# Row sums of seven groups of heads: 32x32 transposes and sums along columns on VectorE in place of a ones matmul

## The chip, the cores and the metric

The kernel runs on one core of one Trainium2 chip. The metric is the device time of one execution in microseconds (us). Of the core's engines five matter here: PE (TensorE, matrix products), ACT (ScalarE, exponentials and copies), DVE (VectorE, additions), POOL (GpSimd, used here to issue DMAs, some of which add to what lies at their destination) and SP (SyncE, which issues the other DMAs). Each engine takes its instructions in the order in which the program issues them.

## The reference

The output mixes attention (A) with a sparse part (B), token by token, by a gate g. Cut to attention, which the change concerns, it is:

```python
def _A_ref(x, wqkv, wo):
    H = 32; Dh = D // H                     # S = 2048 tokens, D = 1024, Dh = 32
    q, k, v = ...                           # x @ wqkv, split into heads
    scores = jnp.einsum("bhqd,bhkd->bhqk", q, k) * (Dh ** -0.5)
    p = _softmax(scores, axis=-1)
    o = jnp.einsum("bhqk,bhkd->bhqd", p, v)
    return o.transpose(...).reshape(B, S, D) @ wo

return g * a + (1 - g) * b
```

The kernel doesn't divide p by its sum. It computes exp(scores), multiplies that with v, and divides afterwards: for each head and each of the 2048 queries it needs the sum of the exponentials over all 2048 keys, the row sum. The change is about how these row sums come about.

## The kernel before

Up to about 628 us of the span the kernel computes q, k, v and part B; from about 1626 us on it multiplies with wo and mixes. Between lies the loop over the 32 heads, eight groups of four (G = 8), which the change touches.

**Tiles of a head.** The keys of a head lie on partitions, 128 at a time: NT = 16 tiles kt, each 128 keys by 2048 queries. `scores` (L1285) makes four products of 512 queries for a tile, each in one bank of `ring`, seven banks of PSUM used in turn. ACT takes 1 to 4 banks at a time and writes exp into P[h, kt] in SBUF (L1294). `pv` (L1306) multiplies P with v on PE. The order is written out: `batches` gives in turn a batch of 9 or 10 products of scores and then products with v some tiles behind. A head has seven batches, and only the third has ten products. A step k = h * 16 + kt stands for one tile; `at(step, f, ...)` puts a piece of other work behind the scores of that step, and in a step such pieces come before `presum`.

**Row sums.** They are sums over partitions and tiles. `presum` adds the tiles of a head into ACC[h] on DVE, and an addition (`add`, L1347) is always two instructions of 1024 columns. Three pairs of tiles, (0, 2), (4, 6) and (8, 10), are first added by a DMA that POOL issues (`accumulate`, L1336: the second onto the first); the sums of the pairs go into ACC by `add_pair` at steps 12 and 17 of the head (counted from its first step) and by a merge at step 21, that is, in tile 5 of the next head. So a head has twelve additions.

For groups 0 to 5 (`FOURS = 6`) the merge and the folds bring four heads into one tile T of 128 partitions, 32 for each head. `merge4` adds the last pair: for the first head of a group straight into T, for the other three its own quarter into T and the rest into ACC. `fold4` and `fold4_end` add the other quarters onto that quarter by DMAs. Then one `head_sums` multiplies T with a matrix of ones on PE (`rowsum`, L1319, into a bank of the ring), ACT copies the sums out (`norm_sums`, L1417), and DMAs carry them to DRAM (SMD) and back into R, 128 partitions by 64 (`load_r`). `norm_r` takes the reciprocal (L1429), multiplies with the gate and writes RD. Groups 6 and 7 do the same for two heads at a time with `merge_even`, `merge_odd`, `fold_even` and `fold_odd`, whose second head also needs two additions for one; heads 30 and 31 have their sums from ACC alone. T is the tile rb0, which the end of the kernel uses again.

**Places of P.** P tiles lie in places that are used again and again: 13 at first, 11 from step 328 (head 20, tile 8), 10 from step 443 (head 27, tile 11), for the others are needed for loads of wo and of other data (`PLACES`). `p_tile` gives each new tile the place that is due first (`until`): 5 steps after a plain tile, 10 after the second of a pair, 14 after the first. ACT can write a tile only when the tile before in its place has been read for the last time: by PE for the product with v, by DVE for the addition, by the DMA of its pair.

Of the kernel before, what the change touches and what calls it, by code (L numbers as in the profile page):

```python
# [19 lines left out]
H = 32  # L20
# [12 lines left out]
def gated_mha_peer_kernel(ctx, tc, xT, wqkv, wv, wo, wq, k12, ug, v, out):  # L33
# [37 lines left out]
    ones4 = const.tile([128, 32], F32, name="ones4")  # L71
    for t, heads in ((ones2, 2), (ones4, 4)):
        nc.vector.memset(t, 0.0)
        for i in range(heads):
            m, w = 128 // heads, 32 // heads
            nc.vector.memset(t[m * i:m * i + m, w * i:w * i + w], 1.0)


    const.tile([128, 120], F32, name="fill")
# [1074 lines left out]
    PLACES = (13, 0), (11, 20 * NT + 8), (10, 27 * NT + 11)  # L1154
# [3 lines left out]
    def p_tile(h, kt):  # L1158
# [4 lines left out]
        i = min((i for i in range(n) if i not in (8, 9) or k < H * NT - 8), key=lambda i: until[i])  # L1163
# [3 lines left out]
                      (wk, f"P{i}") if i < 10 else (keep, ("vhl", "wo_raw2", "wo_raw3")[i - 10]))  # L1167
# [155 lines left out]
    def presum(h, kt):  # L1323
# [14 lines left out]
    def pair(h, i):  # L1338
        return P[h, PAIRS[h == H - 1][i][0]]
# [29 lines left out]
    FOURS = 6  # L1369

    def quarter(i):
        return slice(32 * i, 32 * i + 32)

    def others(q):
        return [quarter(i) for i in range(4) if i != q]

    def merge4(h):
        q = h % 4
        if q == 0:
            add(T, ACC.pop(h), pair(h, -1))  # L1380
        else:
            mine = quarter(q)
            add(T[mine], ACC[h][mine], pair(h, -1)[mine])
            add_pair(h, -1)

    def fold4(h):
        q = h % 4
        if q == 0:
            nc.gpsimd.dma_start(T[up], T[low], accum_op=OP.add)
        else:  # L1390
            a, b, c = others(q)
            nc.gpsimd.dma_start(ACC[h][a], ACC[h][b], accum_op=OP.add)
            nc.gpsimd.dma_start(T[quarter(q)], ACC[h][c], accum_op=OP.add)

    def fold4_end(h):
        q = h % 4
        src = T[quarter(1)] if q == 0 else ACC.pop(h)[others(q)[0]]
        nc.gpsimd.dma_start(T[quarter(q)], src, accum_op=OP.add)

    def head_sums(h, heads=1):  # L1400
        i, = ring_banks(1)
        for ins in rowsum(ring[:, i, :], T if heads > 1 else ACC.pop(h),
                          ones={1: ones, 2: ones2, 4: ones4}[heads]):
# [434 lines left out]
```

## Time and profile before

| | us |
|---|---|
| three runs | 1811.03, 1811.66, 1812.90 (median 1811.66) |
| the execution profiled | 1811.52 |
| its span, first to last instruction | 1809.7 |
| loop over the heads in that span | about 628 to 1626 |

A row of the profile names the line, the engine, the operation and the tiles (written<-read), its shape and count, then the busy time in us, the mean duration of one in ns, and behind a bar the idle time of the engine before such instructions and what ended it. In the timeline a row gives start and duration in us of some instructions in succession that are alike, and in square brackets the idle time before. In rows of stretches the numbers after the length are busy us and counts of PE, PE's weight loads, DVE, ACT and POOL, then the granted clock of PE, the share of the DMA engines and GB/s. A row of waits says who waited for whom, us in total, how often, and the longest. `rb` is T, `wo_raw` and `vhl` are places of P that lie in tiles of these names.

### The profile page before, as it was taken

Reading aid. Unit: us, or ns where it says so; the run is one execution under the profiler, and the core shown is the slowest. Engines: PE = TensorE matmul, PEld = TensorE weight load, DVE = VectorE, ACT = ScalarE, POOL = GpSimd, SP = SyncE. Lnnn points to the kernel's source line nnn. Section 1 sums busy time; section 2 is a strip of 40 time slices with the busy share of each in tenths; the row PEclk is TensorE's granted clock in tenths of the full one; section 3 lists DMA queues with packets and bytes.
Section 4 is the critical chain, followed back from the end, with each engine's and each line's share of the span. In section 5 each row is a group of like instructions: output and inputs, shape, how many; then the busy total and the mean of one; then the engine's idle time right before and its main releaser. Section 6 shows DMA issues by size and latency. Waiting matters only on the chain.

```text
span 1809.7 us, 28079 instructions
## 1 busy us (share of the span) xinstructions
PE 1801.0 (100%) x10631; PEld 1137.0 (63%) x10631; DVE 1503.6 (83%) x1673; ACT 1221.5 (67%) x1613; POOL 262.4 (15%) x314
## 2 busy tenths in 40 slices
PE   9999999999999999999999999999999999999999
PEld 7877777788888745555454555454555545547887
DVE  7868776358988689999989999999899989995674
ACT  4434321211233399999999999999999999993221
POOL 0212000026401211111211111111112010101000
PEclk9999999999999999999999999999999999999999
DMA  6887888723238699999999999999999998957851
GB/s 234 243 284 248 272 267 295 258 79 106 82 129 276 225 217 185 195 198 199 191 202 205 208 209 194 206 184 208 200 202 198 207 199 189 201 130 228 280 168 58
DMA packets 132225, 364.74 MB, mean 202 GB/s; under 512 B 17540, under 2 KB 57876, under 8 KB 106168
## 3 DMA queue, kind: packets, MB, share of 16 engines
q0 software_dynamic: 22064, 136.07, 39.3%
q1 hardware_dynamic: 89864, 190.94, 35.3%
q10 hardware_dynamic: 20160, 35.92, 7.0%
q8 instruction: 84, 1.38, 0.3%
q14 instruction: 53, 0.43, 0.1%
HBM read 169.14 MB, written 72.10 MB: 133 GB/s over the span
## 4 chain that ended last, share of the span: by engine, by line
PE 97%; DMA 2%; ACT 0%; issue 0%; DVE 0%; SPq 0%; ACTq 0%; DVEq 0%
PE ring L1285 29%; PE o L1306 26%; PE bk L157 13%; PE bk L713 10%; PE pa L157 6%; PE bk L760 5%; PE bk L928 2%; PE bk L313 2%; PE pa L1582 2%; PE bk L493 1%; PE bk L397 1%; PE pa L1589 1%; DMA wraw<-in_wqkv 1%; DMA smd<-ssb 1%; PE ring L1319 0%; ACT P L1294 0%
## 5 line engine op out<-in xcount | busy, mean ns | idle before, releaser
L1294 ACT ACTIVATE P<-ring 128x512 f32<-128x512 f32 (+3 forms) x995 | 807.8, 932 | 12.9 <-PE ring L1285 6.7
L1347 DVE TENSOR_TENSOR acc<-acc,P 128x1024 f32<-128x1024 f32 x516 | 596.0, 1219 | 30.5 <-ACT P L1294 29.8
L1306 PE MATMUL o<-P,V 128*32 128x512 f32 (+1 forms) x3896 | 408.7, 540 | 0.0
L1285 PE MATMUL ring<-Q,K 98*128 98x512 f32 x1024 | 269.4, 406 | 0.0
L1285 PE MATMUL ring<-z,z 98*128 98x512 f32 x1020 | 267.5, 406 | 0.1
L1285 PEld LDWEIGHTS ring<-Q,K 98*128 98x128 f32 x1024 | 182.7, 188 | 121.4 <-ACT P L1294 42.1
L1285 PEld LDWEIGHTS ring<-z,z 98*128 98x128 f32 x1020 | 182.1, 188 | 114.6 <-issue 39.5
L1306 PEld LDWEIGHTS o<-P,V 128*32 128x32 f32 x3896 | 108.4, 109 | 203.8 <-issue 179.7
L1336 POOL DMA_DIRECT2D P<-P x78 | 81.4, 1043 | 496.5 <-PE o L1306 190.5
L1347 DVE TENSOR_TENSOR acc<-acc,wo_raw 128x1024 f32<-128x1024 f32 x118 | 139.0, 1220 | 13.4 <-ACT wo_raw L1294 13.4
L1294 ACT ACTIVATE wo_raw<-ring 128x512 f32<-128x512 f32 (+3 forms) x134 | 119.6, 988 | 0.0
L242 ACT ACTIVATE hi<-bk 128x512 fp32r<-128x512 f32 x40 | 23.7, 594 | 116.4 <-PE bk L713 102.2
L713 PE MATMUL bk<-xh,e 128*128 128x512 f32 x384 | 94.2, 394 | 0.0
L713 PE MATMUL bk<-xl,e 128*128 128x512 f32 x384 | 92.2, 389 | 0.0
L713 PEld LDWEIGHTS bk<-xh,e 128*128 128x128 f32 x384 | 71.0, 188 | 22.0 <-issue 3.4
L1347 DVE TENSOR_TENSOR acc<-P,P 128x1024 f32<-128x1024 f32 x60 | 70.8, 1221 | 16.2 <-ACT P L1294 15.9
L255 DVE TENSOR_TENSOR lo<-bk,hi 128x512 fp32r<-128x512 f32 x40 | 27.6, 690 | 67.5 <-ACT hi L242 62.7
L713 PEld LDWEIGHTS bk<-xl,e 128*128 128x128 f32 x384 | 72.1, 188 | 15.0
L103 DVE TENSOR_TENSOR e<-wraw,e 128x512 fp32r<-128x512 f32 (+3 forms) x64 | 54.6, 861 | 27.0 <-ACT e L102 26.7
L102 ACT ACTIVATE e<-wraw 128x512 fp32r<-128x512 f32 (+3 forms) x64 | 44.7, 705 | 37.7 <-DMA wraw<-in_wqkv 22.0
L157 PE MATMUL bk<-xh,e 128*128 128x512 f32 x288 | 68.5, 393 | 0.0
L1306 PE MATMUL o<-wo_raw,V 128*32 128x256 f32 (+1 forms) x632 | 66.6, 496 | 0.0
(300 smaller groups left out, 2377.4 us busy)
## 6 DMA issues: line engine op xcount, KB each, us to landing
P<-P POOLq DMA_DIRECT2D x78, 1024.0 KB, 12.0
wqt<-in_wq SPq DMA_DIRECT2D x26, 1024.0 KB
wraw<-in_wqkv SPq DMA_DIRECT2D x30, 512.0 KB
vhl<-P POOLq DMA_DIRECT2D x13, 1024.0 KB, 13.5
rb<-acc POOLq DMA_DIRECT2D x36, 256.0 KB, 7.2
qdh<-hi ACTq DMA_DIRECT2D x32, 256.0 KB
qdl<-lo ACTq DMA_DIRECT2D x32, 256.0 KB
kdh<-hi ACTq DMA_DIRECT2D x32, 256.0 KB
```

The costliest lines, as they stand in the source:

```text
L102: nc.scalar.activation(hi, src, AF.Copy)
L103: (on or nc.vector).tensor_tensor(out=lo, in0=src, in1=hi.bitcast(F32), op=OP.subtract)
L157: nc.tensor.matmul(ps, self.a[a][i][:, k, :], self.b[b][j][k], start=(not first and k == 0 and i == j == 0), stop=(k == HC - 1 and i == 1))
L313: nc.tensor.matmul(ps[32 * quad:32 * quad + 32, :], kpad[:, quad % 2, i, :], t[:, quad, :], start=(i == 0), stop=(i == 3))
L713: nc.tensor.matmul(ps, t[:, kc // HC, a, kc % HC], x_at(b, n, kc), start=first, stop=last)
L760: nc.tensor.matmul(ps, x_at(a, t // 4, kc)[:, tok], b, start=first, stop=last)
L928: nc.tensor.matmul(p, x_at(a, t // 4, kc)[:, tok], b, start=first, stop=last)
L1285: on_ring(nc.tensor.matmul(ring[:, i, :], K[:98, kt * 128:(kt + 1) * 128], Q[:98, qc * 512:(qc + 1) * 512], start=True, stop=True), i)
L1294: on_ring(nc.scalar.activation(P[h, kt][:, q0 * 512:(q0 + m) * 512].rearrange("p (a m) -> p a m", a=m), ring[:, i:i + m, :], AF.Exp, scale ...
L1306: nc.tensor.matmul(O[h][32 * qc:32 * qc + 32, c0:c1], Vt[g][:, kt, 32 * j:32 * j + 32], p[:, qc * 512 + c0:qc * 512 + c1], start=(kt == 0) ...
L1336: nc.gpsimd.dma_start(P[h, b], P[h, a], accum_op=OP.add)
L1347: nc.vector.tensor_add(out[:, c], a[:, c], b[:, c])
```

## The change

Groups 0 to 6 (`FOURS = 7`) no longer use a ones matmul. Each head is merged into its own ACC with one addition (`merge`), at the same step as before. POOL then issues three DMAs in turn: partitions 64 to 127 are added onto 0 to 63 (`fold64`, step 23 of the head), 32 to 63 onto 0 to 31 (`fold32`, step 27), and the 32 partitions that remain are copied into the head's quarter of T (`collect`, step 31). After the last head of a group, in four successive steps from step 36 of that head, that is, in tiles 4 to 7 of the head after the next, `sum32` transposes a quarter of T's columns in blocks of 32x32 on VectorE (reading T in steps of 64 elements) and adds each 32 columns, which gives R in the layout that `load_r` brought before, without a way over DRAM. `norm_r` follows at step 40; it was at step 52 for groups 0 to 5 and at step 41 for group 6. The matrix `ones4` goes.

Since ACC is held longer, every third head has its ACC in what was the place P9, so P has 12, 10 and 9 places in place of 13, 11 and 10. In group 7, merge and fold of head 28 move three steps back (`late`), since T is still being read by group 6: `merge_even(28)` is now at tile 8 of head 29, behind `norm_r(6)`.

```diff
-    FOURS = 6
...
-    def merge4(h):
-        q = h % 4
-        if q == 0:
-            add(T, ACC.pop(h), pair(h, -1))
-        else:
-            mine = quarter(q)
-            add(T[mine], ACC[h][mine], pair(h, -1)[mine])
-            add_pair(h, -1)
-
-    def fold4(h):
...
+    FOURS = 7
+
+    def fold64(h):
+        nc.gpsimd.dma_start(ACC[h][up], ACC[h][low], accum_op=OP.add)
+
+    def fold32(h):
+        nc.gpsimd.dma_start(ACC[h][:32], ACC[h][32:64], accum_op=OP.add)
+
+    def collect(h):
+        q = 32 * (h % 4)
+        nc.gpsimd.dma_start(T[q:q + 32], ACC.pop(h)[:32])
+
+    def sum32(g, i):
+
+
+        if i == 0:
+            R[g] = wk.tile([128, 128], F32, name="rr", bufs=1)[:, :64]
+        m = slice(16 * i, 16 * i + 16)
+        x = wk.tile([128, 512], F32, name="ssb").rearrange("p (m k) -> p m k", k=32)
+        nc.vector.transpose(x, T.rearrange("p (b m) -> p m b", m=64)[:, m])
+        nc.vector.tensor_reduce(R[g][:, m], x, axis=AX.X, op=OP.add)
...
-    PLACES = (13, 0), (11, 20 * NT + 8), (10, 27 * NT + 11)
+    PLACES = (12, 0), (10, 20 * NT + 8), (9, 27 * NT + 11)
...
-                ACC[h] = wk.tile([128, S], F32, name="acc")
+                ACC[h] = (wk.tile([128, S], F32, name="P9", bufs=1) if h % 3 == 2 else
+                          wk.tile([128, S], F32, name="acc"))
...
             elif g < FOURS:
-                at(base + NT + 5, merge4, h)
-                at(base + NT + 7, fold4, h)
-                at(base + NT + 11, fold4_end, h)
+                at(base + NT + 5, merge, h)
+                at(base + NT + 7, fold64, h)
+                at(base + NT + 11, fold32, h)
+                at(base + NT + 15, collect, h)
             else:
-                at(base + NT + 5, (merge_even, merge_odd)[h % 2], h)
-                at(base + NT + 7, (fold_even, fold_odd)[h % 2], h)
+                late = 3 * (h % 2 == 0)
+                at(base + NT + 5 + late, (merge_even, merge_odd)[h % 2], h)
+                at(base + NT + 7 + late, (fold_even, fold_odd)[h % 2], h)
                 if h % 2:
                     at(base + NT + 14, head_sums, h - 1, 2)
         if j == 3 and g + 1 < G:
-            if g < FOURS:
-                at(base + NT + 18, head_sums, h - 3, 4)
-            at(base + NT + (24 if g < FOURS else 18), load_r, g)
-            at(base + NT + (36 if g < FOURS else 25), norm_r, g)
+            for i in range(4):
+                at(base + NT + 20 + i, sum32, g, i)
+            at(base + NT + 24, norm_r, g)
```

More of the change, by code (lines that the diff above doesn't have):

```diff
@@ L70, in gated_mha_peer_kernel @@
     ones2 = const.tile([128, 32], F32, name="ones2")
[L71 to L79, printed above, removed]
+    nc.vector.memset(ones2, 0.0)
+    for i in range(2):
+        nc.vector.memset(ones2[64 * i:64 * i + 64, 16 * i:16 * i + 16], 1.0)
+    const.tile([128, 152], F32, name="fill")
     ctx.enter_context(tc.tile_pool(name="fillr", bufs=1, side="right")).tile([128, 120], F32, name="fillr")
@@ L1402, in head_sums @@
         for ins in rowsum(ring[:, i, :], T if heads > 1 else ACC.pop(h),
[L1403 removed]
+                          ones={1: ones, 2: ones2}[heads]):
             on_ring(ins, i)
```

19 lines of the change are left out of this document (2 added, 17 removed).

## The prediction

> **What bounds the kernel now.** The page first.
>
> ```profile
> span 1809.7 us, 28079 instructions
> PE 1801.0 (100%) x10631; PEld 1137.0 (63%) x10631; DVE 1503.6 (83%) x1673; ACT 1221.5 (67%) x1613; POOL 262.4 (15%) x314
> PE 97%; DMA 2%; ACT 0%; issue 0%; DVE 0%; SPq 0%; ACTq 0%; DVEq 0%
> ```
>
> The 97% of the chain says TensorE sets the end. The change touches only the loop over the 32 heads (628 to 1626 us), so next comes that loop: waits of ScalarE and of VectorE there, then two stretches of 124 us.
>
> ```profile
> ACT P L1294 <- PE ring L1285: 5.1, 26, 0.3
> DVE acc L1347 <- ACT P L1294: 45.7, 53, 3.1
> 1250.00:1374.00 124.00, 124.00 (x870) 62.29 (x869) 117.00 (x105) 121.81 (x154) 19.46 (x23) 1.00 1.00 202
> 1374.00:1498.00 124.00, 124.00 (x860) 62.34 (x863) 113.68 (x101) 121.38 (x156) 15.40 (x18) 1.00 0.97 204
> ```
>
> Of each four heads PE is busy for all 124 us, ScalarE (x154) for 121.8 and VectorE (x105) for 117.0, at granted clock 1.00. ScalarE waits for nobody but PE. So what PE is spared is gained, as long as VectorE, with 7 us spare in 124, gives back the places of P in time. The chain shows what row sums cost PE: heads begin with the only 10-matmul batch.
>
> ```profile
> 727.77 2.59 PE ring L1285 x10
> 758.72 2.59 PE ring L1285 x10
> 790.54 2.71 PE ring L1285 x10
> 821.62 2.60 PE ring L1285 x10
> 852.58 2.59 PE ring L1285 x10
> L1319 PE MATMUL ring<-rb,ones x72: 592/592/593, 789.5 to 1593.8; 128*32 128x512 f32 x72
> L1417 ACT ACTIVATE ssb<-ring 128x512 f32<-128x512 f32 x10 | 6.0, 599 | 5.0 <-PE ring L1319 5.0
> ```
>
> Distances: 30.95, 31.82, 31.08 and 30.96 us. The row sum at 789.5 lies in the second; that head and the next are longer by 0.87 and 0.13: 1.0 us a row sum. x72 at 8 each are nine row sums of T (a tenth, head 30's, reads ACC).
>
> **The change, part by part.**
>
> *Row sums off PE.* Six of groups 0 to 5 and two of group 6 go; 28/29, 30 and 31 stay. 8 x 1.0 = 8.0 us less on PE; their evacuations (0.6 us each, and 0.5 of waiting) leave ScalarE with them. Gain 8.0.
>
> *VectorE's ledger.* Spared: the second addition of an odd merge; quarter or half the partitions cost as much as 128.
>
> ```profile
> L1347 DVE TENSOR_TENSOR rb<-acc,vhl 32x1024 f32<-32x1024 f32 x18 | 21.2, 1215 | 1.6 <-DMA vhl<-P 1.4
> L1347 DVE TENSOR_TENSOR rb<-acc,P 32x1024 f32<-32x1024 f32 x18 | 21.2, 1213 | 0.3
> L249 DVE TENSOR_REDUCE amax<-hi 128x1 f32<-128x512 f32 x64 | 43.1, 676 | 0.0
> L1645 DVE COPY rb<-pa 128x512 f32<-128x512 f32 x4 | 2.6, 685 | 0.9 <-PE pa L1582 0.9
> L255 DVE TENSOR_TENSOR lo<-c,hi 128x512 fp32r<-128x512 f32 x6 | 7.3, 1214 | 0.1
> L971 DVE TENSOR_SCALAR z<-z 128x1024 f32<-128x1024 f32 x1 | 0.7, 694 | 0.0
> L1429 DVE RECIPROCAL rr<-rr 128x64 f32<-128x64 f32 x8 | 4.4, 548 | 4.3 <-DMA rr<-smd 4.3
> L773 DVE TENSOR_SCALAR eq<-m 128x64 f32<-128x64 f32 x16 | 3.5, 220 | 0.0
> ```
>
> 36 of these and 4 of group 6: 40 x 1.14 (start to start: a row below has 14 in 15.99) = 45.6 us. Added: 28 transposes and 28 reductions. A reduction of 128x512 is 0.68. No transpose is in the trace: between 0.35 (half of L971's 0.694 for twice the columns) and 1.21 (L255, the slowest form of this size); I take 0.69 as the copy of this size has, since a transpose also reads one tensor. A pair is then 1.37 us, 28 of them 38 us, so VectorE's total falls by some 7 us. But it is spread otherwise: 4 x 1.37 = 5.5 us, with reciprocal and product (0.78) right behind, 6.3 in all, now fall between tiles 4 and 8 of one head in four (5, 9, ... 25, 29). The reduction waits for its transpose on the same engine: nothing but additions is queued behind.
>
> *Folds.* Per head three POOL DMAs in a row: 512, 256 and 256 KB, in place of two or three. The next accumulation of P stands behind the first two in POOL's queue, as now.
>
> ```profile
> rb<-rb POOLq DMA_DIRECT2D x9, 512.0 KB, 9.0
> rb<-acc POOLq DMA_DIRECT2D x36, 256.0 KB, 7.2
> 794.12 0.82 POOL L1389 DMA_DIRECT2D rb<-rb  x1 [4.27 <-DVE rb L1347]
> 804.79 0.78 POOL L1398 DMA_DIRECT2D rb<-rb  x1 [7.73 <-DMA rb<-rb]
> ```
>
> Merge 2.3, then 10.7 to the next issue (794.12 to 804.79 shows this very sequence), twice 7.2 and half a microsecond each for issue: 28.4 us. The first transpose comes one head, 30.95 us, after that merge on VectorE: 2.5 us of cover, 0. Should it go, VectorE waits that long with its additions behind. SP loses four stores and a load per group; in the loop nothing on PE waits for a DMA, so 0. Its store of the reciprocals waits for norm_r, now twelve steps earlier; what is queued behind it (loads of V and of the next K and Q) isn't due for seven steps, 13.5 us: 0. Five memsets fewer at the start, at L773's 0.2 us each, beside the first loads: 0.
>
> *Places of P: 13, 11, 10 become 12, 10, 9.* This decides. The planner in p_tile gives the place that is due first; run on paper with the new numbers, up to head 20 every place is free at least 4 us before it is written by the times of now, which covers the 2 to 4 us that VectorE falls behind there. From head 21 on tile 4 takes the place of tile 4 of the head before, which VectorE lets go with add_pair(h, 1); in heads 28, 29 and 31 tile 3 takes it; in head 29 tile 8 takes that of tile 8 of head 28. With the times of now (VectorE's rows, and the ScalarE instruction that will have to wait):
>
> ```profile
> 1287.91 2.35 DVE L1347 TENSOR_TENSOR acc<-P,P 128x1024 f32<-128x1024 f32 x2
> 1293.52 2.36 DVE L1347 TENSOR_TENSOR acc<-acc,P 128x1024 f32<-128x1024 f32 x2 [0.99 <-ACT P L1294]
> 1296.57 2.36 DVE L1347 TENSOR_TENSOR acc<-acc,P 128x1024 f32<-128x1024 f32 x2 [0.68 <-ACT P L1294]
> 1300.30 2.36 DVE L1347 TENSOR_TENSOR acc<-acc,P 128x1024 f32<-128x1024 f32 x2 [1.37 <-ACT P L1294]
> 1304.03 13.71 DVE L1347 TENSOR_TENSOR acc<-acc,P 128x1024 f32<-128x1024 f32 x12 [1.37 <-ACT P L1294]
> 1317.66 2.35 DVE L1347 TENSOR_TENSOR acc<-acc,vhl 128x1024 f32<-128x1024 f32 x2
> 1320.26 1.16 ACT L1294 ACTIVATE P<-ring 128x1024 f32<-128x1024 f32 x1
> ...
> 1505.35 2.36 DVE L1347 TENSOR_TENSOR acc<-acc,vhl 128x1024 f32<-128x1024 f32 x2
> 1506.25 1.93 ACT L1294 ACTIVATE P<-ring 128x2048 f32<-128x2048 f32 x1
> 1522.61 15.99 DVE L1347 TENSOR_TENSOR acc<-acc,P 128x1024 f32<-128x1024 f32 x14 [0.44 <-ACT P L1294]
> 1538.09 1.99 ACT L1294 ACTIVATE P<-ring 128x2048 f32<-128x2048 f32 x1
> 1542.39 2.35 DVE L1347 TENSOR_TENSOR rb<-acc,P 128x1024 f32<-128x1024 f32 x2
> 1547.89 1.90 ACT L1294 ACTIVATE P<-ring 128x2048 f32<-128x2048 f32 x1
> ```
>
> Head 22, tile 4: add_pair(21, 1) ends at 1320.01, the exponential starts at 1320.26: 0.25 to spare. VectorE gets 6.3 more in head 21; its idle time there is 0.99 + 0.68 + 1.37 + 1.37 = 4.4; ScalarE comes 1.0 earlier, as the row sum before tile 4 is gone. 6.3 - 4.4 + 1.0 - 0.25 = 2.65 late.
>
> Head 26, tile 4: the same sum, but whether the 1.0 counts hangs on where VectorE then stands against the row sum; between 1.65 and 2.65 I take 2.1.
>
> Head 28, tile 3: released at 1507.71, wanted at 1506.25: 1.45 late. Head 29, tile 3: 1538.60 against 1538.09: 0.5 late.
>
> Head 29, tile 8: merge_even(28) moves three steps back, behind sum32. After 1542.39 VectorE's order is two pairs (2.7), addition of tile 5 (2.3), two pairs (2.7), addition of tile 7 (2.3), reciprocal and product (0.8), merge (2.3): it ends at 1555.5. The exponential, due at 1547.89, is 7.6 late.
>
> Sum 14.3. ScalarE makes up about 0.3 for each of the five, as its 121.8 of 124 us leave 0.5 per head: 12.8 lost. Total: -8.0 + 12.8 = +4.8.
>
> The execution profiled took 1811.52 us (span and 1.8 around it), 0.14 under the median 1811.66. **1811.66 + 4.8 = 1816.5 us.**
>
> [...] L773 writes single elements 32 bytes apart and takes 0.220, no more than a dense one, but no row reads so; the transpose reads T in steps of 256 bytes. [...]
>
> **The rivals.**
>
> *Dear transposes (slower still).* At L255's 1.21, 0.52 x 4 = 2.1 us more in each late head; heads 22, 26 and 29 pay it in full: +6.2, 1822.7. For it: the read with a stride, which no row of the trace has. Against: nothing in the trace. [...]
>
> *Cheap transposes, or a place that waits by halves (no change).* At 0.35 a pair is 1.03: 1.4 us less in heads 22, 26 and 29, 4.1 in all, 1812.4. And the additions go by halves of 1024 columns: if an exponential of 1024, as in heads 22 and 26, waits only for the half that it overwrites, these two are 1.14 less late: 1814.2; the three others are one instruction of 2048 and gain nothing. For the first: L971's speed with a single source. Against the second: tiles of one place are handed over whole, by my reading of the code.
>
> *VectorE catches up (faster).* Its total falls by 7 us; if that is taken off its lag at the ends of heads, no place is late, and the 8.0 stays: 1803.5. Against: the lag is made between tiles 11 and 15 (seven additions in a row, 15.99 us, while ScalarE needs 7 x 30.95 / 16 = 13.5 us for seven tiles), after the last idle time, and is the same in heads with and without a second merge. It decides from the point where all five places are let go 3 us sooner than reckoned, and the merge 8.
>
> **How the numbers follow.** My forecast 0.44, dear transposes 0.18, cheap ones or halves 0.18, catching up 0.20. The forecast's own range is 1813 to 1820 (each stall by half a microsecond either way, the pair by 0.1). Measurement can tell 0.2%, 3.6 us: below 1808.0 faster, above 1815.3 slower. A tenth of the forecast's cases lies under that: slower 0.40 + 0.18 = 0.58, same 0.18 + 0.04 = 0.22, faster 0.20. The range goes from 1805 (half of the fastest rival left out) to 1826 (a transpose of 1.5).
>
> **What would show it.** Head distances of 30.95 everywhere up to head 21, no 31.8; waits of ScalarE for acc L1347 (none now) near heads 22, 26, 28 and, longest by far, in tile 8 of head 29; a transpose near 0.7; no wait of VectorE for the copies into T. I am wrong if ScalarE still waits for PE alone, if the transposes are far from 0.7, or if they wait for the folds.

## The result and the profile after

The changed kernel takes **1858.8 us** (median of six runs, 1856.07 to 1861.27) where the kernel before takes 1811.55 in the same comparison: 1.0259 times as long, with a 95% interval of 1.0246 to 1.0273. That is 47 us more, ten times the 4.8 that were forecast, and far beyond the range.

The profiled execution took 1856.07 us, 44.6 more than the profiled one before. First its page (head, busy time, shares of the chain):

```profile
span 1854.3 us, 27880 instructions
...
PE 1816.6 (98%) x10567; PEld 1140.4 (61%) x10567; DVE 1502.2 (81%) x1684; ACT 1220.0 (66%) x1608; POOL 267.9 (14%) x328
...
PE 78%; DMA 9%; DVE 5%; issue 5%; ACT 2%; POOL 0%; SPq 0%; ACTq 0%; DVEq 0%; POOLq 0%
```

VectorE's busy time fell by only 1.4 us and TensorE has 64 matmuls less, yet it is busy for 15.6 us more. The chain went from 97% TensorE to 78%, and DMA, VectorE and "issue" now hold 19%. The stretches of the head loop tell where (columns: length, then busy time of PE, PEld, VectorE, ScalarE and GpSimd, then the clock, the DMA share and GB/s):

```profile
656.00:1032.00 376.00, 374.27 (x2593) 187.91 (x2593) 344.74 (x309) 366.47 (x464) 57.62 (x71) 1.00 0.99 201
1032.00:1156.00 124.00, 119.75 (x806) 60.00 (x807) 110.14 (x100) 115.70 (x145) 17.79 (x22) 0.99 1.00 204
...
1280.00:1404.00 124.00, 118.82 (x798) 58.01 (x798) 109.96 (x101) 112.66 (x140) 16.78 (x21) 0.99 0.98 200
...
1528.00:1633.00 105.00, 95.36 (x639) 46.00 (x629) 90.06 (x83) 89.25 (x109) 11.74 (x14) 0.93 0.82 176
```

PE used to be busy for all 124 us of such a stretch. Now it has holes of 2 to 10 us in each of these, and the clock is under 1.00 in three of the four. From the starts of the heads in the two traces the 44.6 us come apart like this: heads 5, 9 and 25 are 1.0 us shorter each (-3.1); the other heads up to 21 are 18.3 us longer (10, 14, 15, 16, 18 and 21 by 2.2 to 4.4 each); heads 22, 26, 28 and 29 are longer by 6.6, 4.2, 0.4 and 13.3 (+24.4); the rest from head 31 on is 5.8 longer; what is left is the start.

Next ScalarE's waits in the loop, which were for PE alone before:

```profile
ACT P L1291 <- PE ring L1282: 16.4, 40, 1.9
ACT P L1291 <- DVE acc L1345: 14.0, 8, 3.3
ACT P L1291 <- DVE rb L1345: 9.1, 1, 9.1
```

and where they stand, in ScalarE's timeline (start, length, and the idle time ahead with what ended it):

```profile
1341.38 5.67 ACT L1291 ACTIVATE P<-ring 128x512 f32<-128x512 f32 x7 [3.29 <-DVE acc L1345]
...
1469.89 5.67 ACT L1291 ACTIVATE P<-ring 128x1024 f32<-128x1024 f32 x7 [3.23 <-DVE acc L1345]
...
1583.78 3.84 ACT L1291 ACTIVATE P<-ring 128x2048 f32<-128x2048 f32 x5 [9.09 <-DVE rb L1345]
```

These are tile 4 of heads 22 and 26 and tile 8 of head 29, the places that the prediction named. VectorE's waits in the loop show what the prediction had named only as a sign of being wrong, waits for the folds:

```profile
DVE ssb L1386 <- DMA rb<-acc: 14.7, 3, 5.6
DVE ssb L1386 <- DMA rb<-P: 4.9, 1, 4.9
...
DVE P L1345 <- DMA P<-wo_raw: 2.5, 1, 2.5
DVE acc L1345 <- DMA P<-wo_raw: 2.2, 2, 1.5
```

Four of its first transposes wait 4.5 to 5.6 us for the copies into T, and additions wait for accumulated tiles: 24 us together, against 1.4 before. Loads are late as well. In heads 15 and 16 the chain that ended last (start, length) runs through three loads on SyncE's queue, and PE waits for the last of them as head 17 begins; no load held PE in the loop before.

```profile
1095.06 21.82 DMA z<-kdh
1116.89 29.30 DMA V<-vd
1146.21 18.64 DMA Q<-shd
```

```profile
PE ring L1282 <- DMA Q<-shd: 2.4, 1, 2.4
```

And this is the long stall of head 29 in windows:

```profile
1571.00:1578.00 7.00, 5.96 (x39) 2.45 (x31) 6.90 (x8) 3.50 (x5) 0.86 (x1) 1.00 0.78 160
1578.00:1586.00 8.00, 0.29 (x1) 0.29 (x2) 5.65 (x7) 2.22 (x2) 0.82 (x1) 0.54 0.36 74
1586.00:1592.50 6.50, 6.50 (x24) 2.50 (x23) 3.58 (x3) 4.47 (x7) 0.00 (x0) 0.51 0.32 63
1592.50:1600.00 7.50, 7.50 (x58) 4.29 (x58) 5.86 (x6) 6.72 (x9) 0.90 (x1) 1.00 0.68 141
```

PE stands still for 8 us, and for the 6.5 us after that it works at clock 0.51: 24 matmuls where the next 7.5 us hold 58. This pause cost more than its length. The trace has seven such stretches at half clock between 943 and 1702 us, 37.5 us in all (the kernel before has none there), which alone can cost up to half of that. The first of them, in head 10, follows two short pauses, of 0.72 and 0.48 us with a single product between them:

```profile
942.22 0.50 PE L1282 MATMUL ring<-z,z 98*128 98x512 f32 x1 [0.72 <-ACT wo_raw L1291]
943.20 1.22 PE L1282 MATMUL ring<-z,z 98*128 98x512 f32 x2 [0.48 <-ACT wo_raw L1291]
```

```profile
943.80:947.20 3.40, 3.40 (x17) 0.91 (x21) 3.40 (x4) 3.08 (x4) 0.34 (x1) 0.50 0.97 206
```

### The profile page after: what moved, and what is told of

It is laid out like the page before. It is cut to its first block, busy times and chain, and to the rows that moved or that the text cites. A ratio compares the mean times of both kernels' runs of the same rounds, so it can differ in the third digit from the quotient of the medians.

```text
span 1854.3 us, 27880 instructions
## 1 busy us (share of the span) xinstructions
PE 1816.6 (98%) x10567; PEld 1140.4 (61%) x10567; DVE 1502.2 (81%) x1684; ACT 1220.0 (66%) x1608; POOL 267.9 (14%) x328
## 4 chain that ended last, share of the span: by engine, by line
PE 78%; DMA 9%; DVE 5%; issue 5%; ACT 2%; POOL 0%; SPq 0%; ACTq 0%; DVEq 0%; POOLq 0%
PE ring L1282 19%; PE o L1303 17%; PE bk L154 12%; PE bk L710 10%; PE pa L154 6%; PE bk L757 5%; DVE acc L1345 3%; PE bk L925 2%; DMA rb<-acc 2%; ACT P L1291 2%; PE pa L1572 2%; PE bk L310 2%; DMA V<-vd 2%; PE bk L490 1%; DMA z<-kdh 1%
## 5 line engine op out<-in xcount | busy, mean ns | idle before, releaser
L1291 ACT ACTIVATE P<-ring 128x512 f32<-128x512 f32 (+3 forms) x992 | 841.9, 968 | 47.6 <-PE ring L1282 16.4
L1345 DVE TENSOR_TENSOR acc<-acc,P 128x1024 f32<-128x1024 f32 x440 | 507.6, 1222 | 35.4 <-ACT P L1291 32.9
L1303 PE MATMUL o<-P,V 128*32 128x512 f32 (+1 forms) x4128 | 434.8, 542 | 0.0
L1282 PE MATMUL ring<-z,z 98*128 98x512 f32 x1020 | 276.5, 411 | 13.2 <-ACT P L1291 6.3
L1345 DVE TENSOR_TENSOR P<-P,P 128x1024 f32<-128x1024 f32 x220 | 255.1, 1221 | 33.7 <-ACT P L1291 30.9
L1303 PEld LDWEIGHTS o<-P,V 128*32 128x32 f32 x4128 | 116.9, 110 | 226.5 <-issue 209.2
L1291 ACT ACTIVATE wo_raw<-ring 128x512 f32<-128x512 f32 (+3 forms) x103 | 84.3, 895 | 7.7 <-PE ring L1282 5.7
L710 PEld LDWEIGHTS bk<-xh,e 128*128 128x128 f32 x384 | 71.0, 188 | 22.0 <-issue 3.4
L1334 POOL DMA_DIRECT2D P<-P x47 | 48.9, 1041 | 105.9 <-PE ring L1282 33.3
L154 PEld LDWEIGHTS bk<-xh,e 128*128 128x128 f32 x288 | 53.5, 188 | 15.1 <-issue 2.5
L154 PE MATMUL pa<-woh,acc 128*128 128x512 f32 x192 | 62.3, 389 | 0.0
## 6 DMA issues: line engine op xcount, KB each, us to landing
P<-P POOLq DMA_DIRECT2D x47, 1024.0 KB, 12.1
wo_raw<-vhl POOLq DMA_DIRECT2D x9, 1024.0 KB, 14.9
```

The costliest lines, as they stand in the source:

```text
L154: nc.tensor.matmul(ps, self.a[a][i][:, k, :], self.b[b][j][k], start=(not first and k == 0 and i == j == 0), stop=(k == HC - 1 and i == 1))
L710: nc.tensor.matmul(ps, t[:, kc // HC, a, kc % HC], x_at(b, n, kc), start=first, stop=last)
L1282: on_ring(nc.tensor.matmul(ring[:, i, :], K[:98, kt * 128:(kt + 1) * 128], Q[:98, qc * 512:(qc + 1) * 512], start=True, stop=True), i)
L1291: on_ring(nc.scalar.activation(P[h, kt][:, q0 * 512:(q0 + m) * 512].rearrange("p (a m) -> p a m", a=m), ring[:, i:i + m, :], AF.Exp, scale ...
L1303: nc.tensor.matmul(O[h][32 * qc:32 * qc + 32, c0:c1], Vt[g][:, kt, 32 * j:32 * j + 32], p[:, qc * 512 + c0:qc * 512 + c1], start=(kt == 0) ...
L1334: nc.gpsimd.dma_start(P[h, b], P[h, a], accum_op=OP.add)
```

## The experiments

Three theories at first. **A:** the new folds load the DMA engines, loads and accumulations land late, and PE pauses. **B:** fewer places of P are enough. **C:** the chain of three transfers holds up GpSimd's queue. A rival to all is that the sums on VectorE do it. The letters are those of the expectations from e5 on; A and C keep their meaning, while B is in e7 the work on VectorE and in e8 anything but the bytes. Every run is set against runs of the kernel before on the same chip (medians of 1809.9 to 1811.0 us). e1 to e4 are one execution each, and those of the changed kernel lie up to 5 us apart.

### What a pause of PE costs: e3_pauses

The kernel before, with more copies of a head's output on ScalarE, so that PE has to wait:

```
-        nc.scalar.activation(o, O.pop(h), AF.Copy)
+        for _ in range(1 + {3: 2, 7: 4, 11: 6, 15: 10, 19: 16, 23: 28}.get(h, 0)):
+            nc.scalar.activation(o, O[h], AF.Copy)
+        O.pop(h)
```

> The kernel before, with 2, 4, 6, 10, 16 and 28 more copies of 0.476 us each on ScalarE at the end of heads 3, 7, 11, 15, 19 and 23, which hold TensorE up. If a pause of TensorE costs itself alone, the heads are longer by these copies less some 0.5 us: 0.5, 1.4, 2.4, 4.3, 7.1 and 12.8. If a pause from some 2.4 us on halves the granted clock for 3.4 us, the longer ones cost 1.7 us more each, and the longest more than that (13.7 us at half clock stood behind the pause of 9 us in the changed kernel): 0.5, 1.4, 4.1, 6.0, 8.8 and 14.5 or more, with as many stretches of clock 0.5.

1861.87 us. The heads behind the added copies grew by 1.3, 5.2, 5.4, 8.5, 12.0 and 19.0 us. The copies stood some 0.6 us apart where 0.476 had been taken: five at the second place, the kernel's own and four more, took 3.12 us. That place in ScalarE's and PE's timeline, and windows of the second, third and fifth (the clock is the column after the brackets):

```profile
879.94 3.12 ACT L1411 ACTIVATE osb<-o 128x512 f32<-128x512 f32 x5
```

```profile
883.60 1.28 PE L1285 MATMUL ring<-z,z 98*128 98x512 f32 x2 [1.91 <-ACT P L1294]
```

```profile
880.00:890.00 10.00, 8.09 (x35) 3.27 (x35) 7.00 (x7) 7.08 (x11) 0.86 (x1) 0.66 0.93 235
1012.00:1022.00 10.00, 7.07 (x36) 2.95 (x36) 5.66 (x6) 8.11 (x13) 0.86 (x1) 0.83 0.84 208
1275.00:1290.00 15.00, 5.55 (x28) 1.49 (x26) 4.76 (x5) 13.09 (x21) 0.86 (x1) 0.66 0.46 111
```

PE stood for 1.91, 2.93 and 9.45 us of these windows, and the clock of the first, 0.66 over 10 us, is what 6.8 us at 0.50 give. So a pause of 1.91 us cost 5.2 us here, and 9.45 us of standing 12.0; where two copies were added the head grew by 1.3 us alone. In the changed kernel the four pauses of 2.02 to 2.54 us each came with 3.4 us at 0.50, so a like length brought a stretch half as long. Nor does the length alone tell whether one follows: there the pauses of 0.72 and 0.48 us, with one product between, were followed by 3.4 us at 0.50, while 0.94 and 0.41 us with one product between, and a single one of 1.33 us, were followed by a clock of 1.00. From which length on the clock falls, no run shows.

### The sums on VectorE: e1_dense, e2_no_sums, e4_sums_later, e7_sums_only

e1_dense: the transposes read 512 columns that lie together (the row sums then stand in another order).

```
-        nc.vector.transpose(x, T.rearrange("p (b m) -> p m b", m=64)[:, m])
+        nc.vector.transpose(x, T[:, 512 * i:512 * i + 512].rearrange("p (m b) -> p m b", b=32))
```

> The changed kernel, but the transposes read 512 columns of T that lie side by side instead of single elements 64 apart; the sums then stand in another order, which changes the output and no duration but that of the transpose. If the step of 64 elements makes the transpose dear, it falls from 1.10 to about 0.69 us, VectorE is spared 28 x 0.41 = 11.5 us, and since late places of P cost more than they are late, the time falls from 1858.8 to 1833-1845. If a transpose of 128x512 takes 1.10 whatever it reads, nothing moves: 1856-1861.

1851.72 us. The transposes' row of the changed kernel, and then that of this run:

```profile
L1386 DVE STREAM_TRANSPOSE ssb<-rb 128x512 f32<-128x512 f32 x28 | 30.9, 1102 | 19.6 <-DMA rb<-acc 14.7 <-DMA rb<-P 4.9
```

```profile
L1386 DVE STREAM_TRANSPOSE ssb<-rb 128x512 f32<-128x512 f32 x28 | 19.7, 704 | 29.8 <-DMA rb<-acc 19.8 <-DMA rb<-P 10.0
```

With steps of 256 bytes a transpose takes 1.102 us, from columns that lie together 0.704: the read costs the difference. But taking it away brought only some 5 to 7 us (41.8 over the kernel before in place of 47.3), hardly more than lies between executions, and the waits for the copies became longer.

e2_no_sums fills the row sums with ones in place of the transposes and reductions:

> The changed kernel without the transposes and reductions (left out: the sums; R is filled with ones instead, so the output is wrong). Merges, folds, copies into T, the twelve places and the late merge of head 28 stay. If the burst of sums on VectorE, with its wait for the copies, is the cause, all of the heads up to 27 take 30.95 us again, what stays is head 29 (5 us) and 2 in head 28, and the time is 1809-1816. If fewer places or the 8 MB of DMA more cost the time by themselves, it stays over 1835 with long heads at 10, 14 to 18 and 22.

1852.5 us. With no sum at all most of the loss is still there, 42.6 us of it in this one execution. VectorE now waits for accumulated tiles:

```profile
DVE P L1345 <- DMA P<-P: 12.0, 3, 5.8
DVE acc L1345 <- DMA P<-wo_raw: 9.7, 6, 2.9
DVE P L1345 <- DMA P<-wo_raw: 8.4, 3, 3.3
DVE acc L1345 <- DMA P<-P: 6.8, 4, 3.0
```

e4_sums_later moves the sums and their scaling of groups 0 to 5 three steps back:

> The changed kernel with sum32 and norm_r of groups 0 to 5 three steps (5.8 us) later, so that the last copy into T has landed. If VectorE's wait for that copy (19.6 us in four groups) makes the lag that the places don't hold, these waits go and with them most of the long heads 10, 14, 18 and 21: 1830-1845. If the 7.6 us of sums make the lag by themselves, the time stays within 4 us of 1858.8 although the waits are gone.

1859.17 us. The waits for the copies fell from 19.6 to 2.0 us and those for accumulated tiles rose from 4.7 to 21; the time did not move. So the wait for the copies is one form of the lateness, not its cause.

e7_sums_only is the other way round: the kernel before, with the row sums of groups 0 to 5 by transposes from its own T.

```
...
-                at(base + NT + 18, head_sums, h - 3, 4)
-            at(base + NT + (24 if g < FOURS else 18), load_r, g)
+                for i in range(4):
+                    at(base + NT + (18, 18, 19, 20)[i], sum32, g, i)
+            else:
+                at(base + NT + 18, load_r, g)
```

> The kernel before with the row sums of groups 0 to 5 made on VectorE by four transposes and four reductions from T, in place of the ones matmul and the loads of its sums; its own merges, folds, and thirteen places stay. Theory A (the folds' traffic, not VectorE's work): heads 5, 9, 13, 17, 21 and 25 fall from 31.93 to about 30.95 us and no head from 4 to 26 gets over 32 us; 1803 to 1815 us. Theory B (7 us of VectorE's work between tiles 4 and 8 of one head in four delays the adds until ScalarE and TensorE pause): heads of 33 us and more in groups 2 to 6, over 1830 us.

1815.29 us, 1.0019 (1.001 to 1.0029). Heads 5, 9 and 25 fell to about 31.0 us, and head 13 too, but heads 18 and 21 grew by 2.7 and 5.1 us, the latter with a pause at half clock. The sums alone thus cost 4 us rather than saving 6; they are a tenth of the loss.

### Places alone: e5_places

```
-    PLACES = (13, 0), (11, 20 * NT + 8), (10, 27 * NT + 11)
+    PLACES = (12, 0), (10, 20 * NT + 8), (9, 27 * NT + 11)
...
```

> The kernel before with the changed kernel's counts of places for the exponentials (12, 10 and 9 in place of 13, 11 and 10) and nothing else. Theory A (extra DMA traffic of the folds delays loads and accumulations, TensorE pauses, and the clock that is granted after a pause is halved): the one place less costs little, within 0 to 4 us of the kernel before, some of it in tile 3 of heads 28 to 30. Theory B (one place less is enough): over 1835 us, with heads of 33 us and more from head 10 on, ScalarE's exponentials waiting for accumulations in groups 2 to 5.

1816.17 us, 1.0024 (1.0014 to 1.0035). Heads 28 and 29 grew by 1.2 and 0.25 us, and the end after head 31 by 3.2; none before did. Theory B, that the places are enough, falls.

### The folds: e6_no_folds, e11_old_folds, e13_half

e6_no_folds is the changed kernel without folds, copies, transposes and reductions; the merges and places stay.

```
...
-                at(base + NT + 7, fold64, h)
-                at(base + NT + 11, fold32, h)
-                at(base + NT + 15, collect, h)
+                at(base + NT + 15, ACC.pop, h)
```

> The changed kernel without the folds by 64 and 32, the copies into T, the transposes and the reductions of the seven groups (the row sums are filled with ones; merges, places and all else stay). Theory A (the folds' DMA traffic): heads 4 to 27 fall to 30.9 to 31.0 us, only heads 28 and 29 stay long (about 32 and 40), the time is 1800 to 1818 us. Theory B (places and accumulators alone): heads 10 to 26 stay long as in the run without the sums, the time is over 1835 us.

1816.9 us, against 1852.5 with the folds and without the sums (e2): there the folds are worth 36 us. Heads 1 to 27 all take 30.9 to 31.0, and VectorE waits for no transfer; head 29, at 39.75, keeps its late merge.

e11_old_folds keeps the sums of groups 0 to 5 and the fewer places and takes the merges and folds of before. Group 6 is wholly as before too, and so is the merge of head 28:

> The changed kernel with the merges and folds of before in groups 0 to 5 (three transfers of 256 KB of which only the last waits for another, the merge writing the head's quarter of T itself) and group 6 as before; the sums on VectorE and the counts of places 12, 10 and 9 stay. If the new folds carry the loss, the costs of the places alone (+5.2) and of the sums alone (+4.3) are left: 1816 to 1826 us. If the sums and the places together make the pauses, whatever the folds: over 1840 us.

1825.04 us, 1.0079 (1.0061 to 1.0098): 34 us less than the changed kernel, but not by the folds alone. With the late merge gone, head 29 takes 31.43 us in place of 44.3. The run to set beside it is e15_six, told below, which has the new folds and the old group 6: 1845.02 us, so that 20 us are left for the new folds and what comes with them (accumulators that come back later, an earlier scaling). Heads 22 and 26 are 5.6 and 3.7 longer than before, as in the changed kernel, and head 21 2.3; the others up to 20 are not.

e13_half folds half of the columns, so that 640 KB move per head in place of 1024, in the same three transfers:

```
-        nc.gpsimd.dma_start(ACC[h][up], ACC[h][low], accum_op=OP.add)
+        nc.gpsimd.dma_start(ACC[h][up, :S // 2], ACC[h][low, :S // 2], accum_op=OP.add)
...
-        nc.gpsimd.dma_start(ACC[h][:32], ACC[h][32:64], accum_op=OP.add)
+        nc.gpsimd.dma_start(ACC[h][:32, :S // 2], ACC[h][32:64, :S // 2], accum_op=OP.add)
```

> The changed kernel with the folds by 64 and 32 over half of the columns only (what this leaves out: the sums of the other half), so 256, 128 and 256 KB per head, 640 KB in place of 1024; the number of transfers, their order, their waits and all work of VectorE stay. Theory A (the bytes on full DMA engines): heads 9 to 22 fall to about 31 us, heads 28 and 29 stay long (32 and 40 to 44): 1816 to 1830 us. Theory C (three transfers in a chain, whatever their size): over 1840 us.

1835.38 us, 1.0137 (1.012 to 1.0154), somewhat over what A expected and under C's bound. Of the long heads only 22, 26, 28 and 29 are left (+5.75, +4.9, +0.3, +13.3); heads 5, 9, 13, 17, 21 and 25 each give their microsecond. The waits of ScalarE:

```profile
ACT P L1291 <- DVE acc L1345: 9.6, 5, 3.3
ACT P L1291 <- DVE rb L1345: 9.1, 1, 9.1
```

In the loop VectorE waits for no transfer at all. This run comes closest to the prediction's own account, with dearer stalls: the changed kernel's instructions and the order of its chain, with 384 KB of accumulation per head less, and 23 us gone. Theory C as it was written, whatever their size, falls. But shorter transfers also shorten the chain: GpSimd's waits for transfers in the loop fall from 258 to 100 us, so this run alone doesn't separate the bytes from a queue that is held.

### The queue and the partitions: e9_spread, e10_rotate

e9_spread puts the three transfers eight steps apart and the sums behind them:

> The changed kernel with the three transfers of a head's folds eight steps (15.5 us) apart in place of four (7.7 us) in groups 0 to 5, and the sums nine steps and their scaling twelve steps later for it: the same bytes, but GpSimd's queue should find each transfer landed before it issues the next. Theory C (GpSimd stands at the second and third transfer until the one before has landed, 10 us and more, and the accumulations of the exponentials behind it are late): the long heads of groups 2 to 5 go, 1815 to 1830 us. Theory A (the bytes: the DMA engines are full and everything on them is late): still over 1840 us.

1862.5 us (two runs, 1849.09 and 1875.91), 1.0286 (1.0218 to 1.0355): not better. GpSimd's waits for transfers fell from 258 to 140 us, but PE then waited for loads, 9.9 us for one of K. It speaks against C, though with two runs that lie 27 us apart, and with each copy now beside the next head's first fold.

e10_rotate folds into the half and the quarter of the partitions in which the head's row of T lies:

```
+        a, b = (up, low) if h % 4 < 2 else (low, up)
+        nc.gpsimd.dma_start(ACC[h][a], ACC[h][b], accum_op=OP.add)
...
+        a, b = (32 * i for i in (h % 4, h % 4 ^ 1))
+        nc.gpsimd.dma_start(ACC[h][a:a + 32], ACC[h][b:b + 32], accum_op=OP.add)
...
+        nc.gpsimd.dma_start(T[q:q + 32], ACC.pop(h)[q:q + 32])
```

> The changed kernel with the folds of a head going to the half and the quarter of the partitions in which the head's row of T lies, so that the last copy stays on its partitions; before, all folds went to partitions 0 to 63 and 0 to 31. Bytes, order and steps are the same. Theory D (one quarter of SBUF's partitions is the narrow place, since all heads fold into it and are copied from it): transfers of 256 KB fall from 7 to 10 us toward 6, the time to under 1835 us. Theories A and C: within 8 us of the changed kernel, over 1848 us.

1850.57 us (two runs), 1.022 (1.0199 to 1.0242). The transfers of 256 KB stayed at 7.6 and 10.0 us. Theory D, one narrow quarter of the partitions, falls.

### Bytes: e8_extra_dma, e14_old_plus, e16_accumulating, e17_plain, e18_old_copy

e8_extra_dma adds to the kernel before, and e14_old_plus to the run with the old folds, 256 KB per head that nothing waits for:

```
...
+    def extra(h):
+        nc.gpsimd.dma_start(SCR[h % 4], Vt[(h + 1) // 4][:32].rearrange("p t m -> p (t m)"))
...
+                at(base + NT + 15, extra, h)
```

> The kernel before with one transfer of 256 KB added on GpSimd's queue in each head of groups 0 to 5, fifteen steps after the head's last tile, from values that are in SBUF already to a scratch in DRAM that nothing reads (so the output is unchanged). It is as many bytes as the folds of the changed kernel move beyond the old ones in a head. Theory A (the added traffic delays the loads and accumulations): heads of 33 us and more from head 10 on, TensorE waiting for loads, and 1825 us or more. Theory B (the transfers are hidden; the delay lies in the order of the folds, the places or VectorE): within 4 us of the kernel before.

> The run with the old folds (sums on VectorE, places 12, 10, 9; 1825 us) with 256 KB per head of groups 0 to 5 added, from values in SBUF to a scratch in DRAM, so that the folds and this move the 1024 KB of the changed kernel's folds; nothing waits for the added transfers, and the output is unchanged. Theory A (the bytes alone, on a kernel with little slack left): 1838 to 1860 us, with long heads from head 10 on. Theory E (the bytes matter only as part of the chain of folds): 1822 to 1832 us.

e8 settles little: eight runs from 1810.05 to 1839.83 us, median 1817.82, while 28 of the kernel before lie between 1809.91 and 1815.11. The ratio, 1.0056 (1.0021 to 1.009), leaves out the two longest, 1838.49 and 1839.83. The profile is one of 1810.05, with no long head, although VectorE waits 13 us for transfers; what held the longer ones isn't on record. It does show that a share of 0.99 was not the engines' end. The same stretch in the kernel before, then in e8:

```profile
656.00:1032.00 376.00, 376.00 (x2628) 189.82 (x2621) 355.36 (x313) 369.63 (x466) 58.38 (x69) 1.00 0.99 197
```

```profile
656.00:1032.00 376.00, 376.00 (x2625) 189.73 (x2627) 354.07 (x312) 369.55 (x468) 64.83 (x81) 1.00 0.99 204
```

e14 is clearer: 1825.52 us (1823.44 to 1828.35) against 1825.04 without the addition. So theory A as it stood, bytes of any kind, falls: as many bytes as the changed kernel moves cost nothing here.

The next two put the whole 1024 KB beside the run without folds (e6), twice 512 KB at NT + 7 and NT + 15, with nothing waiting for them: once as accumulating transfers within SBUF, once as plain writes to DRAM.

```
+                at(base + NT + 7, fold64, h)
+                at(base + NT + 15, fold64, h)
```

The second has, in the place of `fold64`,

```
+    def plain(h):
+        nc.gpsimd.dma_start(SCR[h % 4], ACC[h][low])
```

> The run without folds and sums (1816.9 us) with two accumulating transfers of 512 KB per head of groups 0 to 6, partitions 64 to 127 added into 0 to 63 of the head's accumulator, at the steps NT + 7 and NT + 15: the 1024 KB of the changed kernel's folds. Nothing but the buffer's return waits for them; the sums stay left out (filled with ones). If accumulating bytes beside the accumulations of the exponentials make these late whether anything waits for the folds or not: over 1840 us, with VectorE's waits for transfers of 20 us and more. If the chain of three with its waits on GpSimd's queue is needed: 1815 to 1828 us.

> As the run before it, with two plain transfers of 512 KB from the accumulator to a scratch in DRAM in place of the accumulating ones: the same bytes at the same steps. If bytes of any kind do it: over 1840 us. If plain bytes cost nothing, as the added 256 KB did (1825.5 against 1825.0 us): 1815 to 1825 us.

e16: 1852.67 us, 1.0227 (1.0198 to 1.0256). e17: 1817.87 us, 1.0038 (1.0023 to 1.0052), 1 us over e6's 1816.9. Of e16, the queue's row of the page (packets, MB, busy share of 16 engines), two rows of the transfers (last column: median us to landing) and PE's waits:

```profile
q0 software_dynamic: 22864, 144.45, 39.7%
```

```profile
P<-P POOLq DMA_DIRECT2D x47, 1024.0 KB, 12.3
...
acc<-acc POOLq DMA_DIRECT2D x38, 512.0 KB, 11.9
```

```profile
PE ring L1282 <- DMA Q<-qdh: 14.7, 1, 14.7
PE ring L1282 <- DMA wo_raw<-in_wo: 13.1, 1, 13.1
```

And of e17:

```profile
q0 software_dynamic: 22864, 144.45, 36.6%
```

```profile
P<-P POOLq DMA_DIRECT2D x47, 1024.0 KB, 9.5
...
scr<-acc POOLq DMA_DIRECT2D x38, 512.0 KB, 7.8
```

The same packets and bytes to the last digit, but 39.7% of 1849.9 us is 734 and 36.6% of 1816.4 is 665: the accumulating ones keep the engines busy 69 us longer, a tile's accumulation lands 2.8 us later, and loads come so late that PE stands for 14.7 and 13.1 us. This happens with no chain of three, no sum and nothing waiting for their data. Two limits stand beside it. The runs differ in two things, adding and where the bytes go (SBUF or DRAM), so that neither is shown to be the cause by itself. And e16 doesn't lose its time as the changed kernel does: VectorE waits 3.2 us for transfers where the expectation had 20 and more, and the first accumulation of a head lands 12.1 us after its issue (median of heads 9 to 21) where the changed kernel's takes 14.9. Its 35 us lie in the two waits for loads and the half clock with them, of which the changed kernel has one of 2.4 us, as head 17 begins.

The changed kernel, moreover, accumulates as much as the old folds and adds one plain copy into SBUF. e18_old_copy adds such a copy to e11_old_folds:

```
...
+    def copy(h):
+        a, b, c = others(h % 4)
+        acc = ACC.pop(h)
+        nc.gpsimd.dma_start(acc[b], acc[c])
...
+                at(base + NT + 15, copy, h)
```

> The run with the old folds (sums on VectorE, places 12, 10, 9; 1825 us) with a plain copy of 256 KB per head of groups 0 to 5 within SBUF, at the step NT + 15 at which the changed kernel copies into T: from one used quarter of the accumulator to another, so that no transfer before it and no instruction after it waits for its data. If the third transfer into SBUF is what makes the accumulations late (the added write to DRAM was not): 1840 to 1865 us, the first accumulation of a head landing 16 us after its step. If the order of the new folds does it, with the copy behind two folds in a chain: 1822 to 1832 us, 13 us after its step.

1895.14 us, 1.0468 (1.0451 to 1.0485): 70 us more than without it, where e14 had found nothing for the same bytes to DRAM. But one thing did wait for the copy, against what the expectation says: the accumulator goes back to the next head later.

```profile
DVE acc L1347 <- DMA acc<-acc: 30.6, 12, 6.3
```

These 30.6 us in 12 waits are in the run, so that it doesn't separate the copy's load from the later return. The first accumulation of a head landed 16.5 us after its issue in heads 9 to 21 (median), where it was 12.3 without the copy, 11.7 before and 14.9 in the changed kernel; the addition that needs it stands eight steps, 15.5 us, behind it in the program.

### The late merge and a smaller version: e15_six, e12_three_groups

e15_six is the changed kernel with group 6 summed the old way and the merge of head 28 at its old step. (Head 30 has a merge of its own, which no version moves. Here the merge of head 24 reaches T before the last row sums of group 5 are read, so these are mixed with it; the work is the same.)

```
-    FOURS = 7
+    FOURS = 6
...
-                late = 3 * (h % 2 == 0)
+                late = 0
...
```

> The changed kernel with group 6 summed the old way (ones matmul and old steps for it, and the merges of heads 28 and 30 at their old step, not three steps later). If the stall of 9.1 us in tile 8 of head 29 comes from the later merge of head 28: head 29 falls from 44.3 to about 31.4 us, the stretch of 13.7 us at half clock after it goes, head 27 or 29 gains a row sum of 1 us back: 1843 to 1850 us. If the lateness that was gathered earlier only moves: head 28 or 29 stays over 36 us, 1853 us and more.

1845.02 us, 1.0209 (1.0166 to 1.0252). Head 29 is 31.42 us, and the 13.7 us at half clock are gone: group 6 and the late merge cost some 13 us, as their own term. The other runs lie in the order of what they hold, each over its own kernel before: the places alone 5.2 us (e5), with the sums 14.8 (e11), with the new folds 34.8 (e15), with group 6 and the late merge 47.3 (the changed kernel). The new folds are the largest step.

e12_three_groups is the kernel before with sums on VectorE in groups 0, 1 and 5 alone, where e7 had gained:

> The kernel before with the row sums of groups 0, 1 and 5 alone made on VectorE from T; in the run with six groups the heads behind these three (5, 9 and 25) fell to 30.95 us and none near them grew, while heads 14, 17, 18 and 21 grew behind groups 2 to 4. If a row sum on VectorE pays wherever no weights of the output are being loaded, three heads gain 1.0 us each: 1806 to 1809 us. If VectorE's added work comes out later in the run in another place: 1811 to 1816 us.

1810.7 us against 1810.2, 1.0001 (0.9992 to 1.001). The three heads gained their 1.0 us each, and the part after head 31's start was 2.7 us longer, with 3.4 us at half clock in it. None of the runs beats the kernel before.

## Why the prediction was wrong

*Row sums off PE, -8.0: right.* Where nothing else was late each row sum gave 1.0 us (heads 5, 9, 25; in e13_half six of them, -6.0). The prediction's 30.95 everywhere up to head 21 held in e13_half, not in the changed kernel.

*Transposes at 0.69: wrong by size.* They took 1.10 and lay near the bound of 1.21, because of the strided read (0.704 without). The rival of dear transposes was right in its mechanism, but its 6 us don't carry the result: with dense reads the kernel is still at 1851.72. Reductions were 0.69 as forecast.

*Late places: right in place, too small in price.* ScalarE waited for VectorE just where it was said, in heads 22 (2.65 forecast, 3.29 measured), 26 (2.1; 3.23) and 29, tile 8 (7.6; 9.09, of which the four dearer transposes make 4 x 0.41). The two small ones came as well:

```profile
1532.90 1.88 ACT L1291 ACTIVATE P<-ring 128x2048 f32<-128x2048 f32 x1 [1.39 <-DVE acc L1345]
```

```profile
1565.00 1.88 ACT L1291 ACTIVATE P<-ring 128x2048 f32<-128x2048 f32 x1 [1.29 <-DVE acc L1345]
```

They are tile 3 of heads 28 and 29, forecast at 1.45 and 0.5. Beyond the forecast ScalarE waited for VectorE in heads 9, 14 and 18, up to 1.8 us at a time, where every place was to be free 4 us early. The step that failed here is the pricing of a stall at its own length. The three longer ones pause PE, by 2.02, 2.44 and 8.75 us, and e3_pauses shows what that cost there: 5.2 us for 1.91, 12.0 for 9.45. The five forecast at 14.3 came to 24.4 in these heads, with an earlier wait of 1.9 in head 22; e13_half, where little else is wrong, ends at 1835.4.

*Folds at 0: the step that failed most.* The sum asked only whether the first transpose waits for the chain (28.4 us against a cover of 30.95). The chain was reckoned too short: the copy at its end lands after 10.4 us (median) where 7.2 was taken,

```profile
rb<-acc POOLq DMA_DIRECT2D x19, 256.0 KB, 10.4
```

and VectorE did wait, 4.5 to 5.6 us in four groups. But that wait is not the point, as e4_sums_later shows: without it the time was the same. What was left out is what the folds do to other transfers. A head's first accumulation lands 14.9 us after its issue in place of 11.7, loads come late, and the term that stood at 0 is worth some 20 us (e15_six against e11_old_folds), 23 by halving the folds' bytes (e13_half), 36 by leaving the folds out (e6_no_folds against e2_no_sums). With that falls also "in the loop nothing on PE waits for a DMA, so 0": true before, not after.

*VectorE's ledger.* Its busy total in the page fell by 1.4 us, not by 7. By kind of instruction, the additions that were spared came to 47.6 us (45.6 forecast), the transposes and reductions to 50.1 (38 forecast; the dearer transposes are 28 x 0.41 = 11.5 of the difference): a rise of 2.5. The 4 us between that and the page's total were not followed. *SP's earlier store* was not tried by itself; e6_no_folds keeps it and has no long head up to 27, so it is no cause of its own. *Places in the last head* had no price; with the places alone the part from head 31 on grew by 3.2 us (e5_places). That this run's 5.2 us lie so near the forecast's 4.8 is chance, since no row sum is gained in it and most of its loss lies where the sum had nothing. The direction, slower, came out right, but the largest part of the loss comes from a term that stood at 0.

The rival that VectorE catches up fell: its total hardly dropped, and the late places were all there. So it is shown that the folds carry the largest part of the loss and that plain bytes to DRAM beside the old folds don't. How the folds do it stays open: the copy within SBUF, the accumulating bytes, the chain of waits and the accumulators' later return were not told apart. e18_old_copy points to the copy, but holds the later return too; e16_accumulating shows that accumulating bytes in SBUF cost time, but by late loads.

## What to carry to other kernels

A transfer is not free because its result has time: ask what it makes late for others, and try it with the kind of transfer that the change makes. Here 256 KB per head more to DRAM cost nothing at a DMA share of 0.98 to 1.00 (e14_old_plus), while the new folds cost some 20 us; the share alone told neither. A run that differs in two things gives their sum: the old folds looked worth 34 us, until a run without the late merge showed that 14 of them belong to group 6 and that merge. And a stall that reaches PE is to be priced with the half clock behind it: in e3_pauses 1.3 to 2.7 times the time that PE stood, 1.91 to 9.45 us.

## What the runs showed of the hardware

- A pause of PE of 1.91 us came with a granted clock of 0.66 over 10 us (6.8 us if at 0.50), and the head grew by 5.2 us; where PE stood 9.45 us of a 15 us window, by 12.0 (e3_pauses). In the changed kernel two pauses of 0.72 and 0.48 us with one product between them came with 3.4 us at 0.50, two of 0.94 and 0.41 us and a single one of 1.33 us with none.
- A transpose of 128x512 fp32 on VectorE takes 0.704 us from columns that lie together and 1.102 with steps of 256 bytes.
- With identical packets and bytes, accumulating transfers within SBUF kept the engines busy 734 us and plain writes to DRAM 665 (each a sum over the span, per engine), and the time differed by 35 us. Adding and the destination were not tried apart.
- At a DMA share of 0.99 the engines moved 197 GB/s before and 204 with 256 KB per head more to DRAM, over the same 376 us.
- 256 KB per head more to DRAM cost 0.5 us, a copy of 256 KB within SBUF, with the accumulator held for it, 70.
